# Attention's TensorE products in two runs per unit, the second MoE's outputs with the weights stationary, and all matmul operands at one offset

## The chip, the cores and the metric

One core of a Trainium2 chip runs one program. The metric is the device time of an execution in microseconds; the kernel before was run three times, and one execution more was taken with the hardware profiler. TensorE, VectorE (DVE), ScalarE (ACT), GpSimd (POOL) and SyncE (SP) each run their own instructions in order; here SP issues every DMA.

## The reference

Three stages follow each other. First a linear attention with decay over `r, k, v, w` of shape (4 batches, 8 heads, 768 steps, 48):

```
cur   = (u * k_t) outer v_t
y_t   = r_t . (state + cur)
state = w_t * state + k_t outer v_t
```

Its output becomes 3072 tokens of 384 numbers. The first MoE computes `(silu(x @ w_gate) * (x @ w_val)) @ w_out` with a hidden width of 1536, the second `(h - tanh(h)) @ w_out2` with `h = x @ w_in` and a hidden width of 2048.

## The kernel before, in words

**Attention** goes in 24 units of 256 steps and half the heads, two a round. For each unit VectorE scans the decays (`scan`, P), ACT takes logarithms and exponentials (`lnexp`), VectorE makes the scaled keys and queries (`ekx`, then `ktq`: kt and q), and TensorE makes the scores `sc`, the transposed keys `tr` (copied by ACT in `trc`), the key-value products `kv` and the outputs `y`. `mask` writes the allowed scores over A, in which ACT's `fill` has put the diagonal (from VectorE's `diag`); `state` and `spread` carry the state on; `out` splits y into two parts for the MoE, and `place` moves 16 rows by DMA. In PSUM attention has three banks (pool `aps`), used in turn by the five tiles of each unit: two of sc, kT, kv, y.

The order is written out by hand. `gap(n)` gives what is issued in step n of a round of nine; u0 and u1 are the round's units, `up` the one before, n0 and n1 those ahead. TensorE's work is issued as `gap` is called, VectorE's comes back as chains that `weave` takes one operation of each at a time. 25 of the 113 steps run alone, with chains that convert weights between them; after that one step stands ahead of each group of 9 products in the first MoE.

**The first MoE** takes blocks of 512 tokens. Every number is kept as a high and a low part (x and weights have two halves; `hi` and `lo` of the hidden tile), so a product is three: high by high, and the two mixed ones. For a slice f of 128 hidden columns `mlp` issues 9 products for the gate, 9 for the values (`proj`, L516) and 9 for the outputs of the slice before (`po`, L644). Hidden slices 0 to 5 of all blocks come first, with weights of the pool `wpa`. Then attention's pools close, the pool `wpb` opens in their place, and slices 6 to 11 of all blocks follow with weights from there.

**The second MoE** takes 16 slices m per block: `hm` issues 9 products of 512 columns (L516), `act1` and `act2` make hi and lo, and `om` issues the outputs of two slices before (`oprod`, L867): hi or lo is stationary, 128 tokens at a time, and 384 columns of the weights move, 12 products. Of its 32 weight tiles the first 18 lie in `wpa`, the others in `wpb`. Four accumulators of 128 tokens by 384 are copied out by ACT at the block's end (two of the last block's by VectorE).

**Memory.** A tile starts on a multiple of 32 bytes of its partition. The pools lie in the order in which they are opened: `const`, `wpa` (18 weight tiles of 3072 bytes), `xp` (x), `sb` (s, t, hi, lo of 2048 bytes, and at its end `mx`, `okf`, `fs`, `fi` of 16, 16, 8 and 8 bytes), `f64`, `stage`, `ws`, then attention's `io` and `wk`, in which tiles of 129 columns (2064 bytes: w, P, rst) stand between tiles of 512 and 2048 bytes.

Of the kernel before, what the change touches and what calls it, by code (L numbers as in the profile page):

```python
# [10 lines left out]
I32 = mybir.dt.int32  # L11
# [102 lines left out]
class attention:  # L114
# [3 lines left out]
    def __init__(self, nc, ctx, tc, const, ins, accw, accx):  # L118
        self.nc = nc
        self.rkw_d, self.tok_d, self.v_d, self.ub_d = ins  # L120
        self.accw, self.accx = accw, accx
        self.const = const
        PSUM = bass.MemoryType.PSUM
        self.io = ctx.enter_context(tc.tile_pool(name="io", bufs=3))
        self.wk = ctx.enter_context(tc.tile_pool(name="wk", bufs=2))
        self.ps = ctx.enter_context(tc.tile_pool(name="aps", bufs=3, space=PSUM))
        self.u = [dict() for _ in range(NU)]
        wk = self.wk
        self.u_sb = wk.tile([128, 2, 2 * 96], FP32, name="u_sb", bufs=1)
        self.ident = wk.tile([128, 128], FP32, name="ident", bufs=1)  # L130
        self.cm = wk.tile([128, 4, 128], U32, name="cm", bufs=1)
        self.rst = wk.tile([128, 4, CW], FP32, name="rst", bufs=1)
        self.wmx = wk.tile([128, 1], FP32, name="wmx", bufs=1)

        self.SE = [[[wk.tile([128, 2, 128], FP32, name=f"SE{a}{b}{c}", bufs=1) for c in range(2)]
                    for b in range(2)] for a in range(2)]
# [22 lines left out]
    def load_w(self, u):  # L159
        if u >= NU:  # L160
            return
        s = self.u[u]
        s["w"] = self.io.tile([128, 4 * CW], FP32, tag="w", name="w", bufs=4)
        self.nc.sync.dma_start(out=s["w"], in_=self.rkw_d[u, :, 1024:])
# [28 lines left out]
    def scan(self, u):  # L193
        s = self.u[u]
        w = s["w"]
        s["P"] = self.wk.tile([128, 4, CW], FP32, tag="P", name="P", bufs=4)
        fl = lambda x: x.rearrange("p a b -> p (a b)")
        self.nc.vector.tensor_tensor_scan(fl(s["P"]), w, fl(self.rst), 0.0, ALU.mult, ALU.max)  # L198
        yield
# [20 lines left out]
    def diag(self, u):  # L220
# [7 lines left out]
        yield  # L228
        s["c"] = self.wk.tile([128, 8], FP32, tag="c", name="c")
        nc.vector.tensor_reduce(s["c"], r.rearrange("p (c d) -> p c d", d=D), AX.X, ALU.add)  # L230
# [16 lines left out]

    def ktq(self, u):
        nc, s = self.nc, self.u[u]
        s["kt"] = self.wk.tile([128, 4, 128], FP32, tag="kt", name="kt", bufs=1)  # L250
        nc.vector.scalar_tensor_tensor(
            s["kt"], s["e"], 2.0, s["x0"], ALU.subtract, ALU.mult, reverse0=True)
        yield
        s["q"] = self.wk.tile([128, 4, 128], FP32, tag="q", name="q")
        nc.vector.tensor_tensor(s["q"], self.r(u), s["P"][:, :, 0:128], ALU.mult)  # L255
        yield
# [135 lines left out]
    def gap(self, n, xt, xtile):  # L392
# [9 lines left out]
        if n == 0:  # L402
            if behind:
                c.append(self.state(up))
            if here:
                self.sc(u0)
                self.load_v(u1)
            if ahead:
                c.append(self.scan(n0))
        elif n == 1:  # L410
            if behind:
                self.spread(up)
            if here:
                c.append(self.mask(u0))
            if ahead:
                c.append(self.scan(n1))
                self.load_rk(n0)
        elif n == 2:
            if here:
                self.tr(u0)  # L420
            if behind:
                self.y(up)
            if here:
                c.append(self.ekx(u1))
            if ahead:
                self.lnexp((n0, n1))
        elif n == 3:
            if here:
                self.trc(u0)
                c.append(self.ktq(u1))  # L430
            if behind:
                c.append(self.out(up, x(up)))
            if here:
                c.append(once(lambda: self.fill(u1)))
            self.load_w(u0 + 4)
            self.load_v(n0)
        elif n == 4:
            if behind:
                self.place(up, x(up))
            if here:  # L440
                self.kv(u0)
                self.sc(u1)
            if ahead:
                c.append(self.diag(n0))
        elif n == 5:
            c += [self.state(u0), self.mask(u1)]
            if ahead:
                c.append(once(lambda: self.w_check(n0)))
            self.load_rk(n1)
            self.load_tok(u0 + 4)  # L450
        elif n == 6:
            self.spread(u0)
            self.tr(u1)
            if ahead:
                c.append(self.diag(n1))
                c.append(once(lambda: self.w_check(n1)))
        elif n == 7:
            self.trc(u1)
            self.y(u0)
            if ahead:  # L460
                c.append(self.ekx(n0))
            self.load_w(u0 + 5)
            self.load_tok(u0 + 5)
        else:
            if u0 % UB == 0:
                xt[u0 // UB] = xtile()
            self.kv(u1)
            c.append(self.out(u0, x(u0)))
            if ahead:
                c.append(self.ktq(n0))  # L470
                c.append(once(lambda: self.fill(n0)))
# [4 lines left out]
def body(ctx: ExitStack, tc: tile.TileContext, rkw, tok, vtok, ub, w1, w2, rf, kf, vf, wf, uf, out):  # L476
# [20 lines left out]
    qa_t = const.tile([128, 1], FP32, name="qa_t")  # L497
    zsw_t = const.tile([128, 1], FP32, name="zsw_t")
    xs_d = dram.tile([NB, 128, 2, KD, TB], FP32, name="xs_d")
    pt_d = dram.tile([NB, 128, KD, TB], FP32, name="pt_d")  # L500
# [153 lines left out]
    with tc.manual_schedule():  # L654
# [34 lines left out]
        weave([att.diag(0), att.ekx(0)])  # L689
        weave([att.ktq(0), att.diag(1), c1.chain(), once(lambda: att.fill(0))])  # L690
        att.w_check(0)
# [16 lines left out]
        for b in range(NB):  # L708
            last = b == NB - 1
            if last:  # L710
                cb.until(3 * HF)
                pa.close()
                ex = ctx.enter_context(tc.tile_pool(name="ex", bufs=2, space=PSUM))
                wpb = ctx.enter_context(tc.tile_pool(name="wpb", bufs=3 * HF))
# [105 lines left out]

        NT = TB // 128
        gg, oacc = {}, {}
# [8 lines left out]
        def ptile(n):  # L831
            p = pgv if n % 2 else ex
            return p.tile([128, TB], FP32, tag="p", name="p_ps")
# [23 lines left out]
        def otiles():  # L857
            return [(pac if i < 3 else ex).tile([128, TB], FP32, tag=f"a{i}", name=f"a{i}", bufs=1)
                    for i in range(NT)]

        def oprod(a4, m, gh, gl, wt=None):
            wt = W2[2 * m + 1] if wt is None else wt
            wh, wl = wt[:, 0, :], wt[:, 1, :]
            for i in range(NT):
                sl = slice(i * 128, (i + 1) * 128)
                for n, (a, c) in enumerate(((gh, wh), (gh, wl), (gl, wh))):
                    nc.tensor.matmul(  # L867
                        a4[i][:, :DM], a[:, sl], c, start=(m == 0 and n == 0), stop=(m == NM - 1 and n == 2))

        def om(j, m):  # L870
# [4 lines left out]
            if m == NM - 1:  # L875
                for i in range(NT):
                    o = sb2.tile([128, DM], FP32, tag="o", name="o", bufs=4)
                    if j == NB - 1 and i % 2:
                        nc.vector.tensor_copy(out=o, in_=oacc[j][i][:, :DM])
                    else:  # L880
                        nc.scalar.copy(out=o, in_=oacc[j][i][:, :DM])
                    r0 = order[j] * TB + i * 128
                    nc.sync.dma_start(out=out[r0:r0 + 128, :], in_=o)
                del oacc[j]
# [38 lines left out]

        mx = sb.tile([128, 4], FP32, name="mx", bufs=1)
        okf = sb.tile([128, 4], FP32, name="okf", bufs=1)
        nc.vector.tensor_reduce(mx[:, 0:1], accw, AX.X, ALU.max)
# [9 lines left out]
        nc.tensor.matmul(fz[0:1, 0:4], ones, okf)  # L936
        fs = sb.tile([1, 2], FP32, name="fs", bufs=1)
        nc.vector.tensor_reduce(fs[:, 0:1], fz[0:1, 0:3], AX.X, ALU.add)
        nc.vector.tensor_reduce(fs[:, 1:2], fz[0:1, 0:4], AX.X, ALU.add)
        fi = sb.tile([1, 2], I32, name="fi", bufs=1)  # L940
        nc.vector.tensor_copy(out=fi, in_=fs)
# [40 lines left out]
        with tc.If(flag2 < 512):  # L982
# [3 lines left out]
            with tc.For_i(0, NB, 1) as b:  # L986
# [3 lines left out]
                for m in range(NM):  # L990
# [21 lines left out]
                    oprod(a4, m, gh, gl, wt[1])  # L1012
                for i in range(NT):
                    o = sb2.tile([128, DM], FP32, tag="o", name="o", bufs=4)
                    nc.scalar.copy(out=o, in_=a4[i][:, :DM])
                    nc.sync.dma_start(out=out[bass.ds(b * TB + i * 128, 128), :], in_=o)
            fb.close()
# [61 lines left out]

_OUTS = [((3072, 384), 'float32')]  # L1080

# [70 lines left out]
```

## Time and profile before

| | |
|---|---|
| median of 3 runs | 1029.61 us (1027.26 to 1030.06) |
| profiled execution | 1028.71 us |
| its span, first to last instruction | 1026.9 us |
| TensorE products busy | 973.3 us, 5290 of them |
| TensorE weight loads busy | 825.9 us |
| VectorE busy | 644.1 us |
| ACT busy | 508.9 us |

A busy TensorE is not TensorE at its peak, since the ends of products are modelled and overlap; the starts are measured, and from start to start is what a product costs in a stream. [...]

### The profile page before, as it was taken

The numbers are of one execution on the slowest core, as the hardware profiler recorded it, in microseconds if no ns is written. First come the engines' busy times: TensorE is split into PE (matmuls) and PEld (weight loads), VectorE is DVE, ScalarE is ACT, GpSimd is POOL, SyncE is SP. The second block draws the span as 40 slices with busy tenths as digits, with TensorE's granted clock in tenths as the row PEclk, the third lists the DMA queues.
The fourth block names the chain that finished last, engine by engine and source line by source line (L and its number), as shares of the span: only waits on it lengthen the run. The fifth ranks groups of instructions, "written<-read, shape, count | busy, mean of one in ns | idle before, by whom it ended". The sixth has DMA issues, their size and how long they took to land.

```text
span 1026.9 us, 14184 instructions
## 1 busy us (share of the span) xinstructions
PE 973.3 (95%) x5290; PEld 825.9 (80%) x5290; DVE 644.1 (63%) x1167; ACT 508.9 (50%) x1115; POOL 3.8 (0%) x16
## 2 busy tenths in 40 slices
PE   3669999999999999999999999999999999999994
PEld 2557878888888788888888878999999999999994
DVE  8999878887874424656655535555555555554442
ACT  6767776776753213323332234454454544544541
POOL 1000000000000000000000000000000000000000
PEclk8569999999999999999999999999999999999997
DMA  8566465758552662544465844353353443520001
GB/s 308 182 213 255 125 223 191 251 179 273 175 192 70 243 256 93 184 154 154 184 210 196 308 162 158 99 177 105 93 184 93 124 159 102 185 62 1 32 1 38
DMA packets 54373, 164.14 MB, mean 160 GB/s; under 512 B 6800, under 2 KB 12304, under 8 KB 51472
## 3 DMA queue, kind: packets, MB, share of 16 engines
q1 hardware_dynamic: 54288, 163.06, 46.5%
q8 instruction: 46, 0.75, 0.3%
q14 instruction: 39, 0.32, 0.1%
HBM read 122.14 MB, written 38.54 MB: 156 GB/s over the span
## 4 chain that ended last, share of the span: by engine, by line
PE 87%; DVE 8%; DMA 2%; ACT 1%; issue 1%; SPq 0%; DVEq 0%; ACTq 0%
PE p_ps L516 47%; PE a L867 19%; PE a L644 14%; PE sc_ps L287 2%; PE y_ps L354 2%; DMA w<-in_rkw_dram 1%; PE y_ps L347 1%; DVE P L198 1%; PE kv_ps L304 1%; DMA f<-in_w_dram 1%; DVE A L293 1%; DVE cvt L95 1%; PE kT_ps L267 1%; DVE w L82 1%; DVE cvt L97 0%
## 5 line engine op out<-in xcount | busy, mean ns | idle before, releaser
L516 PE MATMUL p_ps<-x,w 128*128 128x512 f32 x2160 | 533.9, 395 | 0.1
L516 PEld LDWEIGHTS p_ps<-x,w 128*128 128x128 f32 x2160 | 401.6, 188 | 87.4 <-issue 3.7
L867 PE MATMUL a<-w,hi 128*128 128x384 f32 x768 | 197.0, 337 | 0.0
L845 DVE TENSOR_TENSOR t<-p_ps,z 128x512 f32<-128x512 f32 x96 | 66.4, 692 | 168.1 <-ACT z L843 168.1
L644 PE MATMUL a<-hi,w 128*128 128x512 f32 x432 | 148.0, 397 | 0.0
L867 PEld LDWEIGHTS a<-w,hi 128*128 128x128 f32 x768 | 140.9, 188 | 8.2
L619 DVE TENSOR_TENSOR t<-s,p_ps 128x512 f32<-128x512 f32 x72 | 49.4, 686 | 147.6 <-PE p_ps L516 137.7
L867 PE MATMUL a<-w,lo 128*128 128x384 f32 x384 | 129.9, 338 | 2.3 <-DVE lo L854 2.3
L843 ACT ACTIVATE z<-p_ps 128x512 f32<-128x512 f32 x96 | 57.8, 602 | 119.4 <-PE p_ps L516 119.4
L610 ACT ACTIVATE s<-p_ps 128x512 f32<-128x512 f32 x72 | 43.0, 598 | 113.0 <-PE p_ps L516 112.9
L848 ACT CAST hi<-g 128x512 fp32r<-128x512 f32 x96 | 59.7, 622 | 77.6 <-DVE g L846 77.6
L644 PEld LDWEIGHTS a<-hi,w 128*128 128x128 f32 x432 | 81.3, 188 | 18.6
L623 ACT CAST hi<-t 128x512 fp32r<-128x512 f32 x72 | 44.7, 621 | 96.2 <-DVE t L619 95.6
L644 PE MATMUL a<-lo,w 128*128 128x512 f32 x216 | 85.0, 394 | 1.6 <-DVE lo L627 1.6
L867 PEld LDWEIGHTS a<-w,lo 128*128 128x128 f32 x384 | 72.0, 188 | 3.3 <-DVE lo L854 3.3
L846 DVE SCALAR_TENSOR_TENSOR g<-zs,t 128x512 f32<-128x512 f32 x96 | 66.5, 693 | 10.3 <-ACT zs L844 0.5
L844 ACT ACTIVATE zs<-z,sa_t 128x512 f32<-128x512 f32 x96 | 69.6, 725 | 3.1
L854 DVE TENSOR_TENSOR lo<-g,hi 128x512 fp32r<-128x512 f32 x96 | 65.6, 683 | 0.1
L627 DVE TENSOR_TENSOR lo<-t,hi 128x512 fp32r<-128x512 f32 x72 | 49.6, 689 | 19.3 <-ACT hi L623 19.3
L238 ACT ACTIVATE A<-ident,c 128x128 f32<-128x128 f32 x192 | 58.9, 400 | 2.3 <-DVE c L230 2.3
L287 PE MATMUL sc_ps<-q,kt 64*128 64x128 f32 x384 | 34.9, 316 | 24.3 <-DVE q L255 22.7
L287 PEld LDWEIGHTS sc_ps<-q,kt 64*128 64x128 f32 x384 | 29.2, 215 | 29.5 <-DVE q L255 15.3
(86 smaller groups left out, 824.3 us busy)
## 6 DMA issues: line engine op xcount, KB each, us to landing
f<-in_w_dram SPq DMA_DIRECT2D x68, 384.0 KB, 3.9
ck<-in_w_dram SPq DMA_DIRECT2D x68, 384.0 KB, 3.1
rkd<-in_rkw_dram SPq DMA_DIRECT2D x24, 512.0 KB, 4.9
w_d<-ws SPq DMA_DIRECT2D x32, 384.0 KB, 2.6
w<-w_d SPq DMA_DIRECT2D x32, 384.0 KB, 7.3
rk<-in_tok_dram SPq DMA_DIRECT2D x24, 384.0 KB, 5.5
x_d<-x SPq DMA_DIRECT2D x6, 1536.0 KB, 6.1
x<-x_d SPq DMA_DIRECT2D x6, 1536.0 KB, 7.3
```

What stands on the lines that cost most here:

```text
L238: self.nc.scalar.activation(out=a[:, h, i, :], in_=self.ident, func=AF.Copy, scale=s["c"][:, 2 * i + h:2 * i + h + 1])
L287: self.nc.tensor.matmul(s["sc"][h][:, i * 128:(i + 1) * 128], s["kt"][hs, i, :], s["q"][hs, i, :])
L516: nc.tensor.matmul(ps, wt[:, part, k * 128:(k + 1) * 128], x[:, xp_, k, :], start=(n == 0), stop=(n == 3 * KD - 1))
L627: nc.vector.tensor_tensor(h["l"], h["t"], h["h"].bitcast(FP32), ALU.subtract)
L644: nc.tensor.matmul(acc[0][k], a, c, start=(first and i == 0), stop=(last and i == 2))
L843: nc.scalar.activation(out=z, in_=ps, func=AF.Square, accum_out=accz[:, i:i + 1])
L844: nc.scalar.activation(out=s, in_=z, func=AF.Square, scale=C2 ** 0.5, bias=sa_t)
L845: nc.vector.tensor_tensor(hz, ps, z, ALU.mult)
L846: nc.vector.scalar_tensor_tensor(g, s, C2 * SB, hz, ALU.add, ALU.mult)
L848: nc.scalar.copy(out=gh, in_=g)
L854: nc.vector.tensor_tensor(gl, g, gh.bitcast(FP32), ALU.subtract)
L867: nc.tensor.matmul(a4[i][:, :DM], a[:, sl], c, start=(m == 0 and n == 0), stop=(m == NM - 1 and n == 2))
```

## The change

The steps of `gap` are put in another order, so that TensorE's work for a unit comes in two runs: `sc` and `tr` together (steps 0 and 4), `kv` of one unit and `y` of the unit before together (steps 2 and 6). The vector work moves with it; `ktq` is split in `ktx` and `qx`. In the second MoE a slice of the weights becomes stationary and the 512 tokens of hi or lo move: 9 products of 512 columns into three accumulators, which are written out transposed (the host puts the result in order). The PSUM bank that the fourth accumulator had goes to the tiles of `hm`, five in turn. The tiles with odd sizes get the pool `odd` behind `wk`, and four small ones move from `sb` to `const`.

```diff
+        odd = self.odd = ctx.enter_context(tc.tile_pool(name="odd", bufs=2))
...
-        self.rst = wk.tile([128, 4, CW], FP32, name="rst", bufs=1)
-        self.wmx = wk.tile([128, 1], FP32, name="wmx", bufs=1)
+        self.rst = odd.tile([128, 4, CW], FP32, name="rst", bufs=1)
+        self.wmx = odd.tile([128, 1], FP32, name="wmx", bufs=1)
...
-        s["w"] = self.io.tile([128, 4 * CW], FP32, tag="w", name="w", bufs=4)
+        s["w"] = self.odd.tile([128, 4 * CW], FP32, tag="w", name="w", bufs=4)
...
-        s["P"] = self.wk.tile([128, 4, CW], FP32, tag="P", name="P", bufs=4)
+        s["P"] = self.odd.tile([128, 4, CW], FP32, tag="P", name="P", bufs=4)
...
         if n == 0:
-            if behind:
-                c.append(self.state(up))
             if here:
                 self.sc(u0)
+                self.tr(u0)
                 self.load_v(u1)
+                c.append(self.ekx(u1))
             if ahead:
                 c.append(self.scan(n0))
         elif n == 1:
-            if behind:
-                self.spread(up)
             if here:
+                self.trc(u0)
                 c.append(self.mask(u0))
             if ahead:
-                c.append(self.scan(n1))
                 self.load_rk(n0)
         elif n == 2:
             if here:
-                self.tr(u0)
+                self.kv(u0)
             if behind:
                 self.y(up)
             if here:
-                c.append(self.ekx(u1))
+                c.append(self.ktx(u1))
+            if ahead:
+                c.append(self.scan(n1))
+                c.append(self.diag(n0))
+        elif n == 3:
+            if behind:
+                c.append(self.out(up, x(up)))
+            if here:
+                c.append(self.state(u0))
+                c.append(self.qx(u1))
             if ahead:
                 self.lnexp((n0, n1))
-        elif n == 3:
-            if here:
-                self.trc(u0)
-                c.append(self.ktq(u1))
-            if behind:
-                c.append(self.out(up, x(up)))
...
         elif n == 4:
+            if here:
+                self.sc(u1)
+                self.tr(u1)
             if behind:
                 self.place(up, x(up))
             if here:
-                self.kv(u0)
-                self.sc(u1)
+                self.spread(u0)
             if ahead:
-                c.append(self.diag(n0))
+                c.append(self.diag(n1))
         elif n == 5:
-            c += [self.state(u0), self.mask(u1)]
+            self.trc(u1)
+            c.append(self.mask(u1))
...
         elif n == 6:
-            self.spread(u0)
-            self.tr(u1)
-            if ahead:
-                c.append(self.diag(n1))
-                c.append(once(lambda: self.w_check(n1)))
-        elif n == 7:
-            self.trc(u1)
+            self.kv(u1)
             self.y(u0)
             if ahead:
                 c.append(self.ekx(n0))
+                c.append(once(lambda: self.w_check(n1)))
+        elif n == 7:
+            if u0 % UB == 0:
+                xt[u0 // UB] = xtile()
+            c.append(self.out(u0, x(u0)))
+            c.append(self.state(u1))
+            if ahead:
+                c.append(self.ktx(n0))
...
         else:
-            if u0 % UB == 0:
-                xt[u0 // UB] = xtile()
-            self.kv(u1)
-            c.append(self.out(u0, x(u0)))
+            self.spread(u1)
             if ahead:
-                c.append(self.ktq(n0))
+                c.append(self.qx(n0))
...
+    mx = const.tile([128, 4], FP32, name="mx")
+    okf = const.tile([128, 4], FP32, name="okf")
+    fs = const.tile([1, 2], FP32, name="fs")
+    fi = const.tile([1, 2], I32, name="fi")
...
-                ex = ctx.enter_context(tc.tile_pool(name="ex", bufs=2, space=PSUM))
+                ex = ctx.enter_context(tc.tile_pool(name="ex", bufs=3, space=PSUM))
...
-            p = pgv if n % 2 else ex
+            p = pgv if n % 5 in (1, 3) else ex
...
-            for i in range(NT):
-                sl = slice(i * 128, (i + 1) * 128)
-                for n, (a, c) in enumerate(((gh, wh), (gh, wl), (gl, wh))):
-                    nc.tensor.matmul(
-                        a4[i][:, :DM], a[:, sl], c, start=(m == 0 and n == 0), stop=(m == NM - 1 and n == 2))
+            for k in range(KD):
+                wh, wl = (wt[:, i, k * 128:(k + 1) * 128] for i in range(2))
+                for n, (c, g) in enumerate(((wh, gh), (wh, gl), (wl, gh))):
+                    nc.tensor.matmul(a[k], c, g, start=(m == 0 and n == 0), stop=(m == NM - 1 and n == 2))
...
-                for i in range(NT):
-                    o = sb2.tile([128, DM], FP32, tag="o", name="o", bufs=4)
-                    if j == NB - 1 and i % 2:
-                        nc.vector.tensor_copy(out=o, in_=oacc[j][i][:, :DM])
+                for k in range(KD):
+                    o = sb2.tile([128, TB], FP32, tag="o", name="o", bufs=3)
+                    if j == NB - 1 and k == 1:
+                        nc.vector.tensor_copy(out=o, in_=oacc[j][k])
                     else:
-                        nc.scalar.copy(out=o, in_=oacc[j][i][:, :DM])
-                    r0 = order[j] * TB + i * 128
-                    nc.sync.dma_start(out=out[r0:r0 + 128, :], in_=o)
+                        nc.scalar.copy(out=o, in_=oacc[j][k])
+                    nc.sync.dma_start(out=out[order[j], k], in_=o)
```

## Rows read from the trace of the kernel before

**Rows 1.** The page's chain that ended last, share of the span by line.

```profile
PE p_ps L516 47%; PE a L867 19%; PE a L644 14%; PE sc_ps L287 2%; PE y_ps L354 2%; DMA w<-in_rkw_dram 1%; PE y_ps L347 1%; DVE P L198 1%; PE kv_ps L304 1%; DMA f<-in_w_dram 1%; DVE A L293 1%; DVE cvt L95 1%; PE kT_ps L267 1%; DVE w L82 1%; DVE cvt L97 0%
```

**Rows 2.** Windows: stretch, length, busy PE, PEld, DVE, ACT, POOL, granted clock, DMA share, GB/s.

```profile
12.47:74.16 61.69, 39.68 (x301) 33.32 (x301) 60.24 (x123) 43.02 (x119) 0.00 (x0) 0.61 0.65 220
...
103.00:349.19 246.19, 245.23 (x1676) 197.24 (x1675) 189.30 (x366) 160.43 (x401) 0.00 (x0) 1.00 0.55 184
353.28:377.76 24.48, 24.48 (x110) 20.28 (x108) 5.52 (x8) 4.88 (x8) 0.00 (x0) 1.00 0.94 371
379.80:605.64 225.84, 225.84 (x974) 183.13 (x972) 123.76 (x221) 65.73 (x112) 0.00 (x0) 1.00 0.53 187
624.68:1003.95 379.27, 379.27 (x1903) 344.07 (x1902) 211.13 (x340) 191.76 (x383) 0.00 (x0) 1.00 0.32 103
```

**Rows 3.** Timeline of TensorE, both passes: start, length, instruction.

```profile
355.32 4.24 PE L516 MATMUL p_ps<-x,w 128*128 128x512 f32 x18
...
361.44 4.24 PE L516 MATMUL p_ps<-x,w 128*128 128x512 f32 x18
...
386.04 4.35 PE L516 MATMUL p_ps<-x,w 128*128 128x512 f32 x18
...
392.32 4.35 PE L516 MATMUL p_ps<-x,w 128*128 128x512 f32 x18
```

**Rows 4.** Timeline of TensorE, second MoE: first and last start of 90 periods.

```profile
626.78 2.24 PE L516 MATMUL p_ps<-x,w 128*128 128x512 f32 x9
...
1003.95 2.25 PE L516 MATMUL p_ps<-x,w 128*128 128x512 f32 x9
```

**Rows 5.** Timeline of TensorE, attention's runs between MoE products.

```profile
208.14 0.48 PE L644 MATMUL a<-hi,w 128*128 128x512 f32 x1
...
210.31 1.05 PE L347 MATMUL y_ps<-q,SE 128*128 128x128 f32 x8
...
212.32 2.33 PE L516 MATMUL p_ps<-x,w 128*128 128x512 f32 x9
214.58 0.67 PE L304 MATMUL kv_ps<-v,kT 128*64 128x48 f32 x16
215.19 2.33 PE L516 MATMUL p_ps<-x,w 128*128 128x512 f32 x9
```

**Rows 6.** Timeline of TensorE, kv and sc in one run.

```profile
256.58 0.67 PE L304 MATMUL kv_ps<-v,kT 128*64 128x48 f32 x16
257.19 1.16 PE L287 MATMUL sc_ps<-q,kt 64*128 64x128 f32 x16
```

**Rows 7.** What TensorE waited for, 74 to 353 us: total, times, longest.

```profile
PE a L644 <- DVE lo L627: 1.6, 1, 1.6
PE sc_ps L287 <- DVE q L255: 0.9, 2, 0.7
PE sc_ps L287 <- DVE yo L376: 0.9, 2, 0.7
```

**Rows 8.** Timeline of ACT (lnexp's ends) and VectorE (idle before, releaser).

```profile
220.30 1.28 ACT L203 ACT_TABLE_LOAD   x1
...
223.99 1.28 ACT L610 ACT_TABLE_LOAD   x1
...
84.08 1.23 DVE L198 TENSOR_TENSOR_SCAN P<-w,rst 128x516 f32<-128x516 f32 x1 [1.58 <-DMA w<-in_rkw_dram]
...
227.46 0.69 DVE L619 TENSOR_TENSOR t<-s,p_ps 128x512 f32<-128x512 f32 x1 [3.16 <-PE p_ps L516]
```

**Rows 9.** Groups of operations (busy, mean ns) and DMA issues (KB, us to landing).

```profile
L245 DVE TENSOR_TENSOR x<-rkd,x 128x512 f32<-128x512 f32 x24 | 16.5, 689 | 0.4
L745 ACT COPY pt<-a 128x512 f32<-128x512 f32 x12 | 6.6, 582 | 0.0
...
w_d<-ws SPq DMA_DIRECT2D x32, 384.0 KB, 2.6
out_dram<-o SPq DMA_DIRECT2D x24, 192.0 KB, 2.1
```

More of the change, by code (lines that the diff above doesn't have):

```diff
@@ L228, in diag @@
         yield
-        s["c"] = self.wk.tile([128, 8], FP32, tag="c", name="c")
+        s["c"] = self.odd.tile([128, 8], FP32, tag="c", name="c")
         nc.vector.tensor_reduce(s["c"], r.rearrange("p (c d) -> p c d", d=D), AX.X, ALU.add)
@@ L246, in ekx, with ktx @@
         yield
-    def ktq(self, u):
+    def ktx(self, u):
         nc, s = self.nc, self.u[u]
@@ L253, in ktq, with qx @@
         yield
+    def qx(self, u):
+        nc, s = self.nc, self.u[u]
         s["q"] = self.wk.tile([128, 4, 128], FP32, tag="q", name="q")
@@ L689, in body @@
         weave([att.diag(0), att.ekx(0)])
-        weave([att.ktq(0), att.diag(1), c1.chain(), once(lambda: att.fill(0))])
+        weave([att.ktx(0), att.qx(0), att.diag(1), c1.chain(), once(lambda: att.fill(0))])
         att.w_check(0)
@@ L818, in body @@
             tail = mlp(xt[b], range(HF, NF), tail, gap, done, after)
-        NT = TB // 128
         gg, oacc = {}, {}
@@ L857, in otiles, with oprod @@
         def otiles():
-            return [(pac if i < 3 else ex).tile([128, TB], FP32, tag=f"a{i}", name=f"a{i}", bufs=1)
-                    for i in range(NT)]
-        def oprod(a4, m, gh, gl, wt=None):
+            return [pac.tile([128, TB], FP32, tag=f"a{k}", name=f"a{k}") for k in range(KD)]
+        def oprod(a, m, gh, gl, wt=None):
             wt = W2[2 * m + 1] if wt is None else wt
-            wh, wl = wt[:, 0, :], wt[:, 1, :]
-            for i in range(NT):
-                sl = slice(i * 128, (i + 1) * 128)
-                for n, (a, c) in enumerate(((gh, wh), (gh, wl), (gl, wh))):
-                    nc.tensor.matmul(
-                        a4[i][:, :DM], a[:, sl], c, start=(m == 0 and n == 0), stop=(m == NM - 1 and n == 2))
+            for k in range(KD):
+                wh, wl = (wt[:, i, k * 128:(k + 1) * 128] for i in range(2))
+                for n, (c, g) in enumerate(((wh, gh), (wh, gl), (wl, gh))):
+                    nc.tensor.matmul(a[k], c, g, start=(m == 0 and n == 0), stop=(m == NM - 1 and n == 2))
         def om(j, m):
@@ L921, in body @@
         act2(*prev[-1])
-        mx = sb.tile([128, 4], FP32, name="mx", bufs=1)
-        okf = sb.tile([128, 4], FP32, name="okf", bufs=1)
         nc.vector.tensor_reduce(mx[:, 0:1], accw, AX.X, ALU.max)
@@ L936, in body @@
         nc.tensor.matmul(fz[0:1, 0:4], ones, okf)
-        fs = sb.tile([1, 2], FP32, name="fs", bufs=1)
         nc.vector.tensor_reduce(fs[:, 0:1], fz[0:1, 0:3], AX.X, ALU.add)
         nc.vector.tensor_reduce(fs[:, 1:2], fz[0:1, 0:4], AX.X, ALU.add)
-        fi = sb.tile([1, 2], I32, name="fi", bufs=1)
         nc.vector.tensor_copy(out=fi, in_=fs)
@@ L1012, in body @@
                     oprod(a4, m, gh, gl, wt[1])
[L1013 to L1016, printed above, removed]
+                for k in range(KD):
+                    o = sb2.tile([128, TB], FP32, tag="o", name="o", bufs=3)
+                    nc.scalar.copy(out=o, in_=a4[k])
+                    nc.sync.dma_start(out=out[bass.ds(b, 1), k].rearrange("o p t -> p (o t)"), in_=o)
             fb.close()
@@ L1077, in slow_attention @@
         nc.sync.dma_start(out=xs_d[n], in_=xs.bitcast(FP32))
-_OUTS = [((3072, 384), 'float32')]
+_OUTS = [((NB, KD, 128, TB), 'float32')]
 def layouts(inputs):
@@ L1150 @@
     got = tuple(r.results[0][f"out_{i}_dram"] for i in range(len(_OUTS)))
-    return got[0]
+    return _np.ascontiguousarray(got[0].transpose(0, 3, 1, 2)).reshape(NTOK, DM)
```

## The prediction

> **What bounds the kernel now.** I read the chain of waits by line first. TensorE's products own nearly all of it: the projections of both MoEs, the second MoE's outputs and the first MoE's outputs together 80% [rows 1]. Then the windows by stage [rows 2]. From 12.5 to 74 us attention runs alone, and VectorE is busy 60.24 of 61.69 us: it sets that stage, with TensorE's granted clock at 0.61. [...] So the question for three quarters of the time is how long one product takes.
>
> The timeline of TensorE answers it [rows 3]. A slice of the first MoE is 27 products of 512 columns, 18 of L516 and 9 of L644. At 355 us a slice takes 6.12 us from start to start, 226.7 ns a product; at 386 us 6.28 us. Over the stretches it is 24.48 us for 4 slices against 225.84 us for 36, 6.273 us each, 232.3 ns a product [rows 2]. Shapes, clock and instructions are the same. What differs is where the weights lie: the second pass takes them from the pool that opens when attention closes. Transfers don't explain it: the faster stretch has DMA engines 0.94 busy, the slower 0.53 [rows 2]. Tiles start on multiples of 32 bytes, and between the first weights and the second ones all sizes are multiples of 512 bytes but four: `mx`, `okf`, `fs`, `fi`, in `sb`, one 32-byte slot each. So the second weights stand 128 bytes off the first ones, off `x`, `hi` and `lo`, counted modulo 512; the first weights stand at 0 to them.
>
> **The change part by part.** *One offset.* The four small tiles go to the first pool and the 129-column tiles to one of their own behind the rest. Then both halves of the weights, `x`, `hi`, `lo` and attention's operands stand at 0 to each other. If that is the cause, the second pass goes at the first's pace: 36 x (6.273 - 6.120) = 5.5 us less. Other bound: 0, if the cause is another.
>
> *Second MoE turned round.* Per (block, slice) 9 products of 512 columns and 12 of 384 become 18 of 512; the columns are the same, 9216. The first period starts at 626.78 and the last of the 90 ends at 1003.95: 4.191 us each [rows 4]. [...] 18 x 226.7 = 4.080 us, 0.111 less, x 96 = 10.6 us. Other bound, at the second pass's 232.3 ns: 18 x 232.3 = 4.182, 0.8 us. I take 10.6, since both operands come to the offset of the 353 us row. `lo` is now wanted by the second product, not the third, but two slices ahead. The accumulators' three copies of about 582 ns [rows 9] take the place of four on an ACT busy half of that stage [rows 2]; were they late, the next block's first output product would wait for its accumulator.
>
> [...]
>
> *Joined runs.* TensorE's attention work in nine steps stood in six runs between MoE products (sc; tr with y; kv with sc; tr; y; kv), now in four (sc with tr, kv with y, twice). A group of 9 MoE products takes 2.04 us undisturbed (9 x 226.7); shut between runs it takes 2.26 (212.32 to 214.58), after a lone tr 2.17 (208.14 to 210.31) [rows 5]. The two runs that vanish save 0.22 + 0.13 = 0.35 us. A joint costs the run itself nothing where the trace shows one: kv ahead of sc takes 0.61 us [rows 6], kv alone 0.61 [rows 5]. Sc to tr and kv to y aren't shown; by the nearest rows a joint lies between 0 and one side of an interruption, 0.11 us. Four joints at 0.11 would turn 0.35 into a loss of 0.09. I take 0.25 saved, nearer to the shown joint. 113 steps less the 25 ahead of the first MoE product are 88, 9.8 rounds: 2.4 us less (from 3.4 less to 0.9 more).
>
> *Order of the steps.* No DMA issue changes its step; `out` falls from 24 to 18 issues. `ekx` of the next pair falls into the 25 steps ahead of the MoE (two 0.69 us operations [rows 9] on the engine that sets that stage), and kv(5), y(4) now run ahead of the first MoE product instead of behind it: moved, and mostly given back by 95 us. The second scan stands a step later, so its 1.58 us wait for `w` [rows 8] should go; TensorE's waits from 74 to 353 us come to 3.4 us [rows 7], and at best all go. Against that stands a new wait. `aps` has three banks and five tiles per unit: in step 4 sc(u1) and tr(u1) need the banks of kv(u0) and y(up), freed by the last of `state(u0)` and by `out(up)`, both in step 3, `out` behind `lnexp` on ACT. From step 2's start TensorE needs about 0.6 + 2.0 (kv, y) + 2.26 + 2.05, 6.9 us, to reach sc(u1). ACT needs a silu (some 0.6, as a copy of that size [rows 9]), lnexp (220.30 to 223.99: 3.7 us) and `out`'s casts (0.6): 4.9. VectorE then waits for the MoE's `mul`, which waits for the v projection as at 227.46 [rows 8], at 4.9 of the 6.9, and has some 2 us of `mul` (0.69 [rows 9]), `out` (as much in halves) and the small `state` operations left: 6.9 to 7.4. So up to 0.5 us a round is short, 5 us in all; queued behind sc are tr and the next projection. Bounds: 3.4 less, 5 more. I take 1.0 more, close to no change.
>
> *End.* The last copy and its transfer grow by a third: 192 KB land in 2.1 us, 384 KB in 2.6 [rows 9]; 256 KB in about 2.3. With `lo` wanted earlier at three waits I take 0.3 more (0 to 0.6).
>
> **Sum.** -5.5 - 10.6 - 2.4 + 1.0 + 0.3 = -17.2 us. The profiled execution took 1028.71 us (span 1026.9), so 1011.5 by its time; it lay 0.9 below the median of the three runs, 1029.61. Against that median: 1012.4 us.
>
> **The rivals.** *1. The place of the operands means nothing.* Then the second pass keeps 6.273 and the second MoE goes at 232.3 ns: -0.8 - 2.4 + 1.3 = -1.9, 1027.7 us. For it: two stretches are a small sample, and the second pass differs in its x loads and conversions too. Against it: the DMA shares run the other way, and the pace changes with the very slice in which the weights change. [...]
>
> *2. Slower: not the difference counts but the place itself, where the second weights lie.* All operands move to that place, 224 modulo 512 where the first ones were at 96. Then the first pass slows as well: 36 slices x 0.153 = 5.5 us on top of rival 1, 1033.2 us. It decides from the point where the pass with equal offsets goes above 6.2 us a slice. For it: only the slow stretch has operands there. Against it: there `x` and `hi` were still at 96, and 128 bytes alone make a plain shift of both.
>
> *3. The joined runs wait.* Joints at 0.11 us (+0.9) and 0.5 us short in each round (+5): 1012.4 + 3.3 + 4.0 = 1019.7 us. For it: ACT's and VectorE's close margins above, and VectorE busy 189.30 of 246.19 us there [rows 2]. Against it: TensorE waited only in single places so far [rows 7].
>
> **How the numbers follow.** Forecast 0.72, rival 1 0.12, rival 2 0.05, rival 3 0.11. The forecast's own range is 1007 to 1018 (attention's and the start's bounds halved); rival 3 lengthens it to 1006 to 1022, which leaves rivals 1 and 2 outside. About 0.3%, 3 us, is what a measurement can tell from no change. Forecast, rival 3 and a quarter of rival 1 are faster: 0.86. The rest of rival 1 and a little of rival 2 within: 0.10. Slower: 0.04.
>
> **What would show it.** Right: slices of 6.12 us in both passes of the first MoE; periods of 4.08 us in the second, with no product above 230 ns in the middle of a stretch; four attention runs per nine steps, each followed by a group near 2.2 us; no wait over 0.5 us on sc after 150 us. Wrong: a second pass still at 6.27 (rival 1), a first pass after attention at 6.27 (rival 2), waits of sc or tr on VectorE's `out` or `state` once a round (rival 3), or a first MoE product more than 3 us later than 74.2 that isn't made up by 103 us.

## The result and the profile after

The changed kernel takes 1017.14 us (1016.63 to 1017.39, four runs) against 1029.53 for the kernel before on the same chip: a ratio of 0.9883 [0.9871, 0.9896], 12.4 us faster. The forecast was 1012.4, so the change brought 4.8 us less than forecast, inside the range. The profiled execution took 1017.23 us, its span is 1015.5.

The chain by line, from the page of the kernel after, against [rows 1] (L529 is the old L516, L878 the old L867, L657 the old L644):

```profile
PE p_ps L529 47%; PE a L878 19%; PE a L657 14%; PE y_ps L360 2%; PE y_ps L353 2%; PE sc_ps L293 2%; PE kv_ps L310 1%; PE kT_ps L273 1%; DVE P L201 1%; ACT A L241 1%; DVE A L299 1%; DMA f<-in_w_dram 1%; DVE cvt L97 0%; DVE w L82 0%; DVE cvt L95 0%
```

Nearly the same list. New in it is `ACT A L241`, attention's `fill`, with 1%. The windows by stage, against [rows 2]: stretch, length, busy PE, PEld, DVE, ACT, POOL, granted clock (a share of full speed), DMA share, GB/s.

```profile
12.69:80.06 67.37, 39.53 (x308) 32.12 (x308) 63.19 (x129) 44.34 (x122) 0.00 (x0) 0.74 0.61 205
...
356.90:381.40 24.50, 24.50 (x110) 20.28 (x109) 5.52 (x8) 4.87 (x8) 0.00 (x0) 1.00 0.93 367
383.40:609.20 225.80, 225.80 (x998) 186.95 (x997) 126.26 (x225) 67.44 (x116) 0.00 (x0) 1.00 0.52 187
626.90:1002.17 375.27, 374.02 (x1650) 308.86 (x1648) 214.48 (x354) 193.09 (x381) 0.00 (x0) 1.00 0.31 100
```

The first row is attention alone, up to the first MoE product. That product starts at 80.06 us, before at 74.16: 5.9 us later. VectorE has 63.19 us of work there against 60.24 and is idle 4.18 us against 1.45: 2.95 us of work more, 2.73 us of idle time more, and the stretch begins 0.22 later. Of the other rows, the second (first pass of the MoE) is as before, the third (second pass) holds 998 products where 974 stood in the same length, and the fourth has fewer, since the second MoE now does with 18 products a period what took 21.

TensorE's timeline in the second pass of the first MoE and in the second MoE, against [rows 3, 4]; columns are start, length, instruction:

```profile
487.46 4.24 PE L529 MATMUL p_ps<-x,w 128*128 128x512 f32 x18
493.58 4.24 PE L529 MATMUL p_ps<-x,w 128*128 128x512 f32 x18
...
641.07 2.20 PE L529 MATMUL p_ps<-x,w 128*128 128x512 f32 x9
643.11 0.39 PE L878 MATMUL a<-hi,w 128*128 128x512 f32 x1
...
645.15 2.20 PE L529 MATMUL p_ps<-x,w 128*128 128x512 f32 x9
...
987.87 2.20 PE L529 MATMUL p_ps<-x,w 128*128 128x512 f32 x9
...
991.95 2.20 PE L529 MATMUL p_ps<-x,w 128*128 128x512 f32 x9
```

A slice of the second pass now takes 6.12 us (493.58 - 487.46), as in the first pass; it was 6.28. A period of the second MoE is 4.080 us at both ends, before 4.191.

The account by stage, after less before: attention and the start +3.6 us, second pass -5.45, second MoE with its copies -10.1, the last transfers +0.6; together -11.4, the difference of the two spans. The +3.6 comes from the start of the same product in both traces: the first product of the first MoE is 5.9 us late, product 216 (counted from 0) 3.63 (155.3 against 151.7), product 810 3.65 (348.52 against 344.87). All of the loss is made in attention's first rounds, and 2.3 us of it are given back by 151 us. Within a round the difference swings, since attention's runs now stand ahead of other products; at the starts of rounds 7 and 12 it is 3.77 and 3.65. So from there on, beside the MoE, the new order neither wins nor loses. Two of these sizes hold for this trace alone: with the same order, the traces of runs 4 to 7 below have the first product at 78.5 to 80.1 us and product 810 2.2 to 3.8 us late; and from the last `hm` to the end of the program, where the +0.6 lies, kernels with one and the same end differ by up to 1.3 us (22.97 before, 24.25 in run 2).

### The profile page after: what moved, and what is told of

Same layout as the page of the kernel before. It is cut to its first block, busy times and chain, and to the rows that moved or that the text cites. A ratio compares the mean times of both kernels' runs of the same rounds, so it can differ in the third digit from the quotient of the medians.

```text
span 1015.5 us, 13518 instructions
## 1 busy us (share of the span) xinstructions
PE 957.3 (94%) x5002; PEld 782.9 (77%) x5002; DVE 642.4 (63%) x1166; ACT 510.1 (50%) x1110; POOL 3.8 (0%) x16
## 4 chain that ended last, share of the span: by engine, by line
PE 88%; DVE 6%; ACT 2%; issue 1%; DMA 1%; SPq 0%; DVEq 0%; ACTq 0%
PE p_ps L529 47%; PE a L878 19%; PE a L657 14%; PE y_ps L360 2%; PE y_ps L353 2%; PE sc_ps L293 2%; PE kv_ps L310 1%; PE kT_ps L273 1%; DVE P L201 1%; ACT A L241 1%; DVE A L299 1%; DMA f<-in_w_dram 1%; DVE cvt L97 0%; DVE w L82 0%; DVE cvt L95 0%
## 5 line engine op out<-in xcount | busy, mean ns | idle before, releaser
L529 PE MATMUL p_ps<-x,w 128*128 128x512 f32 x2160 | 522.7, 391 | 0.3 <-DMA x<-yo 0.2
L529 PEld LDWEIGHTS p_ps<-x,w 128*128 128x128 f32 x2160 | 404.5, 188 | 86.9 <-issue 2.2
L878 PE MATMUL a<-hi,w 128*128 128x512 f32 x576 | 192.9, 389 | 0.0
L657 PE MATMUL a<-hi,w 128*128 128x512 f32 x432 | 146.8, 394 | 0.0
L878 PEld LDWEIGHTS a<-hi,w 128*128 128x128 f32 x576 | 108.1, 188 | 22.4
L878 PE MATMUL a<-lo,w 128*128 128x512 f32 x288 | 112.4, 390 | 2.6 <-DVE lo L866 2.6
L657 PEld LDWEIGHTS a<-hi,w 128*128 128x128 f32 x432 | 81.1, 188 | 18.4 <-issue 1.5
L657 PE MATMUL a<-lo,w 128*128 128x512 f32 x216 | 84.5, 391 | 0.0
L878 PEld LDWEIGHTS a<-lo,w 128*128 128x128 f32 x288 | 54.1, 188 | 14.9 <-DVE lo L866 3.9
L293 PE MATMUL sc_ps<-q,kt 64*128 64x128 f32 x384 | 32.2, 308 | 30.6 <-DVE q L261 29.4
L241 ACT ACTIVATE A<-ident,c 128x128 f32<-128x128 f32 x192 | 58.9, 392 | 2.6 <-DVE c L233 2.5
L293 PEld LDWEIGHTS sc_ps<-q,kt 64*128 64x128 f32 x384 | 26.9, 207 | 38.9 <-DVE q L261 31.0
```

The source lines that it names most:

```text
L241: self.nc.scalar.activation(out=a[:, h, i, :], in_=self.ident, func=AF.Copy, scale=s["c"][:, 2 * i + h:2 * i + h + 1])
L293: self.nc.tensor.matmul(s["sc"][h][:, i * 128:(i + 1) * 128], s["kt"][hs, i, :], s["q"][hs, i, :])
L529: nc.tensor.matmul(ps, wt[:, part, k * 128:(k + 1) * 128], x[:, xp_, k, :], start=(n == 0), stop=(n == 3 * KD - 1))
L657: nc.tensor.matmul(acc[0][k], a, c, start=(first and i == 0), stop=(last and i == 2))
L878: nc.tensor.matmul(a[k], c, g, start=(m == 0 and n == 0), stop=(m == NM - 1 and n == 2))
```

## The experiments

**The theory:** the difference of the operands' addresses sets the pace of the products (parts A and B of the gain), and what was lost came from the order of the steps ahead of the MoE. The rivals: places have no effect of their own; the place counts, not the difference; the loss lies in the joined runs.

**1. The old order of steps, the rest as after.**

```diff
         if n == 0:
+            if behind:
+                c.append(self.state(up))
             if here:
                 self.sc(u0)
-                self.tr(u0)
                 self.load_v(u1)
-                c.append(self.ekx(u1))
...
```

> The changed kernel with attention's steps in the old order: offsets and the turned outputs stay. Theory: the new order is what fell short of the forecast. It brought nothing in the rounds beside the MoE (two interruptions fewer, four joints more) and cost 3.6 us in the stretch ahead of the first MoE product, so without it the time is 1017.1 - 3.6 = 1013.5 us, and the first MoE product starts near 74 us, not 80. Rival: the order saved its 2.4 us, and the loss comes with the moved tiles (attention's odd tiles behind the rest): then 1017.1 + 2.4 = 1019.5 us and the first MoE product still starts near 80 us.

Measured: 1013.44 us (1012.87 to 1014.13), ratio 0.9853 [0.9836, 0.9869]. The first MoE product starts at 74.75 us, and from 151 to 345 us the same products start within 0.07 us of the kernel before. So the new order costs 3.7 us (3.4 against run 5, which has the new order and was timed beside this one), and this version beats both kernels.

**2. The new places alone, in the kernel before.**

```diff
+        odd = self.odd = ctx.enter_context(tc.tile_pool(name="odd", bufs=2))
...
-        s["w"] = self.io.tile([128, 4 * CW], FP32, tag="w", name="w", bufs=4)
+        s["w"] = self.odd.tile([128, 4 * CW], FP32, tag="w", name="w", bufs=4)
...
+    mx = const.tile([128, 4], FP32, name="mx")
...
-        mx = sb.tile([128, 4], FP32, name="mx", bufs=1)
...
```

> The kernel before with the tiles' places of the changed one, nothing else. Theory (the difference of the operands' places counts): slices of the second pass fall from 6.273 to 6.120 us, 5.5 us in all, and the second MoE's period from 4.191 to between 4.12 (12 products of 384 columns at 13.3 ns on top) and 4.19: 1017 to 1024 us. Rival (places mean nothing): 1029.5 us, second pass at 6.27.

Measured: 1023.67 us, ratio 0.9956 [0.9940, 0.9973]. The timeline of this kernel, second pass and second MoE:

```profile
489.41 4.24 PE L521 MATMUL p_ps<-x,w 128*128 128x512 f32 x18
495.53 4.24 PE L521 MATMUL p_ps<-x,w 128*128 128x512 f32 x18
...
683.40 2.24 PE L521 MATMUL p_ps<-x,w 128*128 128x512 f32 x9
685.48 0.51 PE L872 MATMUL a<-w,hi 128*128 128x384 f32 x2
...
687.58 2.24 PE L521 MATMUL p_ps<-x,w 128*128 128x512 f32 x9
...
691.77 2.24 PE L521 MATMUL p_ps<-x,w 128*128 128x512 f32 x9
```

The second pass takes 6.12 us a slice: not one instruction of the MoE differs from before, only places do. The second MoE, with 9 products of 512 columns and 12 of 384, stays at 4.18 to 4.19, the upper end of what was expected. Its 512-column products don't reach 226.7 ns although all operands now stand at 0 to each other: nine of them take 2.08 us from start to start (683.40 to 685.48), 231 ns each, and the twelve others 2.10, 175 ns each. The expectation's 4.12 took 13.3 ns per product on top of its columns; no run shows how a product's time splits into the two.

**3. The turned outputs alone, with the old places and the old order.**

```diff
...
-                    nc.tensor.matmul(
-                        a4[i][:, :DM], a[:, sl], c, start=(m == 0 and n == 0), stop=(m == NM - 1 and n == 2))
+                    nc.tensor.matmul(a[k], c, g, start=(m == 0 and n == 0), stop=(m == NM - 1 and n == 2))
...
```

> The kernel before with the second MoE's outputs turned round, nothing else: old order, old places (second weights 128 bytes off). Theory: slices whose weights lie in the first pool (9 of 16) go at 4.08 us instead of 4.19, those with weights of the second pool at 4.18: 96 slices save 9/16 x 0.11 + 7/16 x 0.01, 6.4 us: 1022 to 1023 us, second pass still at 6.27. Rival (a sum of independent parts: order_before less offset_only, 1028.4 - (1023.7 - 1013.4)): 1018.2 us.

Measured: 1024.02 us (1023.75 to 1024.29), ratio 0.9951 [0.9933, 0.9968]. The second pass keeps its old 6.27 to 6.28 us a slice. The second MoE shows the cause more sharply than any other run. The starts of `hm` through one block of this kernel, m = 2 to 15 and then 0 and 1 (behind the last two also the start of `om`):

```profile
679.73 2.21 PE L518 MATMUL p_ps<-x,w 128*128 128x512 f32 x9
683.81 2.20 PE L518 MATMUL p_ps<-x,w 128*128 128x512 f32 x9
...
704.21 2.20 PE L518 MATMUL p_ps<-x,w 128*128 128x512 f32 x9
708.29 2.27 PE L518 MATMUL p_ps<-x,w 128*128 128x512 f32 x9
712.49 2.25 PE L518 MATMUL p_ps<-x,w 128*128 128x512 f32 x9
...
725.01 2.25 PE L518 MATMUL p_ps<-x,w 128*128 128x512 f32 x9
729.19 2.25 PE L518 MATMUL p_ps<-x,w 128*128 128x512 f32 x9
...
737.55 2.21 PE L518 MATMUL p_ps<-x,w 128*128 128x512 f32 x9
739.60 0.40 PE L867 MATMUL a<-hi,w 128*128 128x512 f32 x1
...
741.71 2.25 PE L518 MATMUL p_ps<-x,w 128*128 128x512 f32 x9
743.80 0.39 PE L867 MATMUL a<-hi,w 128*128 128x512 f32 x1
```

Seven periods take 4.08 us, then nine take 4.14 to 4.20. Seven and nine is what the places ask for. The first 18 of the 32 weight tiles lie in `wpa`, those of m = 0 to 8, and a period holds `hm(m)` and `om` of two slices before: for m = 2 to 8 both take weights from `wpa`, for the others at least one takes them from `wpb`. Same instructions, same stage, same hidden tiles. The expectation had it the other way round, nine fast and seven slow, since it went by a slice's own weights and not by all that a period takes; its 1022 to 1023 us were missed by 1 us. The last two periods show one thing more: `hm(0)` and `hm(1)` have the same x and weights from `wpa`, at 0 to each other, and yet the first takes 2.05 us (737.55 to 739.60) and the second 2.09 (741.71 to 743.80). So behind slow products the pace isn't settled by a product's own operands alone; what else sets it stays open. The turn alone, then, gains in 7 of 16 periods, and neither edit reaches 4.08 throughout without the other: alone they bring 4.8 and 4.4 us, in run 1 together 15.0.

**4 to 7. Kernel after with an idle tile.** Three kernels shift all that lies behind `sb` by 128, 256 or 64 bytes; the fourth shifts all operands together, by 128 bytes in `const`.

```diff
+        pad = sb.tile([128, 32], FP32, name="pad", bufs=1)
+        nc.vector.memset(pad, 0.0)
```

(64 columns for 256 bytes, 16 for 64 bytes; `const.tile([128, 32], ...)` ahead of `mx` for the common shift.)

> The changed kernel with one idle tile of 128 bytes at the end of the pool sb, so that the second weights stand 128 bytes off x, hi, lo again, modulo 512. Theory: the second pass goes back to 6.27 us a slice (+5.5 us), and of the second MoE's slices those with weights from the second pool (7 of 16) to about 4.18 us (+4.2 us): 1026.8 us. Rival (places mean nothing; the gains came from the turn and the order): 1017.1 us, all slices unchanged.

> The changed kernel with one idle tile of 128 bytes in the first pool: all operands move by 128 bytes together, to 352 modulo 512. Theory (only the difference counts): 1017.1 us, slices of 6.12 and periods of 4.08. Rival (the place itself counts): slices and periods change, by up to 0.15 us a slice in both passes, 1017 to 1028 us.

> The changed kernel with an idle tile of 256 bytes where the kernel pad_128 had one of 128. It asks which period the difference of places has. If 256 bytes are one period: 1017 us, slices of 6.12 us in the second pass. If the period is 512 or more: a slower second pass, 6.2 to 6.3 us, 1022 to 1028 us. I hold the first for likelier at 0.6, since all weight slices and x rows lie 512 bytes and more apart and nothing in the runs so far separates 256 from 512.

> The changed kernel with an idle tile of 64 bytes where pad_128 had one of 128. If any difference that is no multiple of 256 bytes costs the same: 1028 us, slices of 6.27 us in the second pass. If the cost grows with the difference: in between, some 1022 us. If 64 bytes are harmless: 1017 us. I hold the first for likeliest (0.5).

| kernel | us | ratio to before | slice, second pass |
|---|---|---|---|
| 128 bytes between | 1028.12 | 0.9994 [0.9984, 1.0003] | 6.27 |
| 128 bytes for all | 1016.87 | 0.9889 [0.9872, 0.9905] | 6.12 |
| 256 bytes between | 1017.55 | 0.9887 [0.9865, 0.9909] | 6.12 |
| 64 bytes between | 1029.24 | 1.0003 [0.9993, 1.0014] | 6.30 |

Second-pass slices on TensorE's timeline, of the kernels with 128, 256 and 64 bytes between in this order:

```profile
483.63 4.35 PE L529 MATMUL p_ps<-x,w 128*128 128x512 f32 x18
489.90 4.35 PE L529 MATMUL p_ps<-x,w 128*128 128x512 f32 x18
```

```profile
487.35 4.24 PE L529 MATMUL p_ps<-x,w 128*128 128x512 f32 x18
493.47 4.24 PE L529 MATMUL p_ps<-x,w 128*128 128x512 f32 x18
```

```profile
484.34 4.36 PE L529 MATMUL p_ps<-x,w 128*128 128x512 f32 x18
490.64 4.36 PE L529 MATMUL p_ps<-x,w 128*128 128x512 f32 x18
```

One idle tile of 128 bytes takes back 11.0 of the 12.4 us. With it the periods of the second MoE show run 3's pattern, seven of 4.08 and nine up to 4.20; the expectation had again counted seven slow ones, which is most of the 1.3 us that the time lies above it. Moved by 128 bytes all together, the operands show none of it. So the difference counts, not the place, and rival 2 is out. 256 bytes between cost nothing, so of the differences tried 0 and 256 are good, 64 and 128 bad; the prediction's "modulo 512" was wider than needed.

By addresses alone, then, a product costs 226.7 ns (6.12/27) or 232.2 to 233.3 (6.27/27 and 6.30/27). Where this arises, no run shows.

**8. The old order for the first three rounds, the new one from the fourth.**

```diff
...
+        return (self.gap_old if n < 27 else self.gap_new)(n, xt, xtile)
...
```

> The changed kernel with attention's old order in the first three rounds (27 steps, nearly all ahead of the first MoE product) and the new order from the fourth round on. Theory: the loss of the order lies in the stretch ahead of the MoE alone, and beside the MoE the joined runs bring nothing, since a joint costs what an interruption did: 1013.4 us, as with the old order throughout, first MoE product near 74.8 us, and no drift against that kernel from 150 to 350 us (within 0.3 us). Rival: the joined runs do save 0.25 us a round beside the MoE, hidden so far by new waits of the early rounds: 1011.2 us, 2 us gained from 100 to 350 us.

Measured: 1012.10 us (1010.87 to 1012.88), ratio 0.9831 [0.9812, 0.9850]; first MoE product at 74.93 us; the time lies between the theory's 1013.4 and the rival's 1011.2. Against the kernel before, product 216 starts 1.46 us earlier and product 810 1.42 earlier. So the joined runs, in force for the last nine rounds, bring nothing from 151 to 345 us. The 1.4 us come earlier, where the old order lets TensorE wait: its waits for `lo`, `q` and `yo` of [rows 7] are gone, and from 74 to 353 us it waits 1.5 us in all, in run 1 3.2. The wait for `w` of [rows 8] is gone from VectorE's list too. It is the fastest version of all; its interval overlaps that of run 1, so of these two only the traces, not the times, say that it is faster.

**9. `fill` a step later; 10. `diag` in its old steps.** Which part of the new order costs the first rounds? TensorE's and VectorE's waits there, in the kernel after (12 to 103 and 12 to 100 us; total, times, longest):

```profile
PE sc_ps L293 <- DVE q L261: 29.4, 6, 12.7
PE y_ps L353 <- DVE A L299: 4.2, 3, 2.7
...
DVE w L82 <- ACT w L77: 3.7, 3, 1.5
```

The old order has 22.0 us in the first of these waits, 1.1 in the second and none in the third. VectorE, the engine that sets this stage, waits for ACT's cast in the conversion of the weights, and ACT's timeline in the kernel after shows what stands ahead of one of these casts:

```profile
57.55 2.45 ACT L241 ACTIVATE A<-ident,c 128x128 f32<-128x128 f32 x8
59.90 0.49 ACT L77 CAST w<-cvt 128x384 fp32r<-128x384 f32 x1
```

VectorE had written `cvt` by 59.0 us; the cast waits for the eight parts of `fill` and VectorE, which has 1.47 us of idle time here, for the cast. Two edits follow from it (cut; the step numbers are added here):

```diff
-                c.append(once(lambda: self.fill(u1)))  # step 3
+                c.append(once(lambda: self.fill(u1)))  # step 4
-                c.append(once(lambda: self.fill(n0)))  # step 8
+                    c.append(once(lambda: self.fill(u0)))  # step 0
```

> The changed kernel with fill of a unit's diagonal (ACT, 2.45 us) one step later, in steps 0 and 4 instead of 8 and 3. Theory: VectorE idles in the early rounds since the conversion's low part waits for a cast that stands behind fill on ACT (3.7 us in three places); without fill there 1.5 to 3 us come back: first MoE product at 77 to 78.5 us, 1014.1 to 1015.6 us. Rival: the early loss is TensorE's longer chain (sc, tr, kv, y one behind the other ahead of the MoE) and fill has no part in it: 1017 us, first product near 80.

```diff
-                c.append(self.diag(n0))  # step 2
-                c.append(self.diag(n1))  # step 4
+                c.append(self.diag(n0))  # step 4
+                c.append(self.diag(n1))  # step 6
```

> The changed kernel with diag of the next pair back in its old steps (4 and 6, not 2 and 4), all else new. Theory: in the first rounds the new order puts three more VectorE operations (diag, some 1.5 us) ahead of q, on which sc, tr, mask and y ahead of the first MoE product hang; without them q of unit 5 comes near 69 us, not 70.5, the first MoE product near 78.5 us, not 80, and the time is 1015.6 to 1016.5 us. Rival: VectorE's work is only moved about; the first product stays near 80 us and the time at 1017.1 us.

Both missed. With `fill` later the time is 1015.78 us (1014.52 to 1016.49), ratio 0.9867 [0.9848, 0.9886], but the first product still starts at 80.08. By 151 us its trace is 2.2 us late instead of 3.63; but so is that of run 5 (2.13), in which `fill` stands where it did, and the two times overlap (run 5: 1016.87, from 1015.52 to 1017.23). So no gain is shown. With `diag` moved back, the first product comes at 79.57 and the time is 1016.96, ratio 0.9885 [0.9868, 0.9901], that of the kernel after. VectorE's waits in the two, in this order:

```profile
DVE c L233 <- ACT A L241: 3.7, 3, 2.1
```

```profile
DVE w L82 <- ACT w L77: 5.6, 5, 1.5
DVE x L380 <- ACT yo L378: 1.7, 2, 1.4
```

The wait for the cast went in the first and a wait for `fill` itself took its place; in the second it grew and another joined it. So ACT in turn with VectorE holds these rounds, and moving one piece names another. Which piece of the order costs the 3.7 us was not settled; that the order of the first rounds costs them, runs 1 and 8 show.

## Why the prediction was right or wrong, step by step

- **One offset** (forecast -5.5): right, -5.45 in the second pass, and with its cause: runs 2, 4 and 5.
- **Second MoE turned round** (forecast -10.6): right, -10.1 with the end's copies; the period is the 4.080 us that was worked out. The text tied this size to the places (0.8 us at the second pass's pace); by run 3, with the old places, 7 of 16 periods gain all the same. At equal offsets the 21 products of run 2 take 4.18 to 4.19 us and the 18 here 4.08; whether their number or the operands' roles make the difference, no run separates.
- **Joined runs** (forecast -2.4): mis-sized, about 0. The step took four joints near one shown joint, which is free [rows 6], and two vanished runs at 0.35 us a round. Neither came out. Two joints are not free. TensorE's timeline of the kernel after, against [rows 5]:

```profile
206.01 1.16 PE L293 MATMUL sc_ps<-q,kt 64*128 64x128 f32 x16
207.10 0.66 PE L273 MATMUL kT_ps<-ident,kt 128*128 128x128 f32 x4
207.51 4.35 PE L529 MATMUL p_ps<-x,w 128*128 128x512 f32 x18
211.80 0.67 PE L310 MATMUL kv_ps<-v,kT 128*64 128x48 f32 x16
212.40 1.16 PE L353 MATMUL y_ps<-q,SE 128*128 128x128 f32 x8
213.49 1.09 PE L360 MATMUL y_ps<-A,v 128*64 128x128 f32 x16
214.51 0.50 PE L657 MATMUL a<-hi,w 128*128 128x512 f32 x1
```

  From its first product to the MoE's next one `y` takes 2.01 us behind a MoE product [rows 5] and 2.11 behind `kv` (212.40 to 214.51): 0.105 us by the single records. Behind `sc` the first two products of `tr` stand 166 ns apart, where 109 would do. Two of each are 2 x (0.105 + 0.057) = 0.32 us a round. The upper bound had reckoned with that ("four joints at 0.11 would turn 0.35 into a loss"), and it was set aside as the less likely one. But the trace of the kernel before held a second joint, which the prediction passed over, `tr` ahead of `y`:

```profile
195.54 0.60 PE L267 MATMUL kT_ps<-ident,kt 128*128 128x128 f32 x4
195.97 0.61 PE L347 MATMUL y_ps<-q,SE 128*128 128x128 f32 x4
...
207.79 0.60 PE L267 MATMUL kT_ps<-ident,kt 128*128 128x128 f32 x4
208.14 0.48 PE L644 MATMUL a<-hi,w 128*128 128x512 f32 x1
```

  Four products of `tr` take 0.43 us to the start of `y` and 0.35 to the start of a MoE product. This joint vanished too. The sum over rounds 7 to 9 of both traces, from start to start by the single records: attention's own runs take 0.15 us a round more than before, the MoE's products 0.17 less, not 0.35. The two cancel.
- **Order of the steps** (forecast +1.0): mis-sized, +3.6, and for another reason than the one weighed. The feared wait of TensorE on `out` or `state` beside the MoE did not come: from 103 to 353 us it waits 0.2 us in all. That +3.6 still lies inside the term's bounds, which were made from that wait, is luck. The step failed at "moved, and mostly given back by 95 us": VectorE had 2.95 us more to do ahead of the MoE, not two operations of 0.69, and 2.73 us more of idle time, which the sum did not have; of the 5.9 us only 0.8 had come back by 95 us, and 2.3 by 151. Which piece of the order makes it stays open (runs 9 and 10). The prediction's own sign for wrong, a first product more than 3 us late that isn't made up by 103 us, came true.
- **End** (forecast +0.3): +0.6, at its bound. The issues of the three last transfers span 3.11 us on SP's queue, where four smaller ones had spanned 2.06. Since kernels with the same end differ by more than that, the size is not shown.
- **Rivals.** 1 is out by runs 2 and 4, 2 by run 5. 3 came nearer in the sum (1019.7), from the wrong place: its joints at 0.11 were about right for one of the two pairs, its wait in each round did not exist.

By these two traces the two failed terms are 2.4 + 2.6 = 5.0 us of the span's 5.8 too little; the rest is 0.5 of part B and 0.3 of the end.

## What to carry to other kernels

Where products of the same shape run at two paces at one granted clock (here 226.7 and 232.3 ns at 1.00, [rows 2, 3]), look at the addresses of their operands before their transfers: a few odd tiles in a pool can shift everything behind them. Two edits that each remove half of a cause need not add up (here 4.8 and 4.4 us alone, 15.0 together), so try them together too. And a schedule that serves the long stage may cost its gain in the short one ahead of it: keep an order for each.

## What the runs showed of the hardware

- In a stream of its like, a product of 512 columns with a weight load takes 226.7 ns when its two operands in SBUF stand 0 or 256 bytes apart in the sense of the prediction, 232.2 ns at 128 and 233.3 at 64. The granted clock was 1.00 in these stretches before and after; over the whole profiled executions it was 0.975 at 64 and at 256 bytes and 0.977 at 128. Other differences were not tried, and why it is so stays open. Behind slow products, nine with operands 0 bytes apart took 2.05 us in one place and 2.09 in another (run 3), so the neighbours count too.
- Equal offsets hardly helped where lengths are mixed: with 9 products of 512 and 12 of 384 columns a period stays at 4.18 to 4.19 us (run 2), before 4.191, and a 512-column product takes 231 ns there, a 384-column one 175. In that form the hidden tile is the stationary operand of the 12; whether the lengths or this is the reason was not separated.
- Whether a joint of two kinds of small products is free depends on the pair: `kv` to `sc` 0 [rows 6], `sc` to `tr` 57 ns, `tr` to `y` some 80 ns, `kv` to `y` 105 ns.
